# Four of six modulation vectors made by VectorE instead of TensorE in a fused transformer block

## Chip, cores and metric

One core of a Trainium2 chip (trn2). The metric is the device time of one execution in microseconds (us). PE is TensorE, DVE is VectorE, ACT is ScalarE, POOL is GpSimd and SP is SyncE, which here only issues DMAs.

## What is computed

A block of 2048 tokens of width 512: attention over a sliding window of 256 keys with 32 heads of 16, then a gated feed-forward layer of width 1792. Both halves are steered by six vectors of 512 numbers that are made from one condition `c`.

```
mod = (_silu(c) @ w_mod).reshape(1, 6, 1, -1)      # c: 1 x 512, w_mod: 512 x 3072
sa, ca, ga, sb, cb, gb = mod[:, 0], ..., mod[:, 5]
h = _layernorm(x) * (1 + ca) + sa
x = x + ga * attention(h, wqkv, wo)
h = _layernorm(x) * (1 + cb) + sb
x = x + gb * swiglu(h, w1, w3, w2)
```

In the kernel the six vectors are numbered j = 0 to 5 in this order. Vectors 0 and 1 are needed at once, since the first LayerNorm feeds all that follows. Vectors 3 and 4 are needed in the second half of the run, and the gates 2 and 5 when `wo` and `w2` are multiplied by them (the first of these some 130 us into the run).

## The kernel before

The features lie on the 128 partitions in KC = 4 chunks (k = 0 to 3), the tokens in NB = 4 blocks of 512 (b = 0 to 3). All matrix products are made from float32 parts in three passes (`hT` and the weights have a high and a low part each).

The run has an opening of about 57 us, then a long attention phase, then the feed-forward phase. Only the opening is touched by the change. In it the kernel loads x, makes the LayerNorm of each block of tokens (`ln1`, line 632), turns the normed tokens to features on partitions (PE, line 649), applies scale and shift and splits into two parts (`mod_split`, lines 362 to 368: ACT makes `h`, DVE makes both parts of `hT`), makes the values (`values`, line 663, PE products at line 671) and the first queries and keys (`unit_a`, line 442, PE products at line 451), and sends the rows of queries and keys by DMA into the tile `ring` (line 474), in three row groups r = 0, 1, 2 of two DMAs each. Group 0 is cut from the product by ACT (line 460), groups 1 and 2 are finished by two subtractions on POOL (line 469). The scores of a unit (line 504, on PE) read all three groups from `ring`; DVE takes the largest of each row (line 511).

The order is written out by hand. Each step is handed to `at(t, fn)` with a time in an arbitrary unit, the list is sorted, and the functions are called in that order (lines 725 to 727). So each engine has one fixed sequence of instructions, and it waits in place for whatever the next one needs. The dictionary `W` on line 44 holds the times: `mr` and `mm` for the modulation, `ml` for its loads. Each DMA queue is one such sequence too: a DMA whose data is not ready holds back every DMA that SP has behind it.

A modulation vector is made in four steps by `modulation(j, s, t0, at)` (line 578). `row` (line 586): four products of the condition (32 equal columns, `sc32`) with the four chunks of the weight, each on its own 32 rows of the result, 8 matmul instructions since each float32 product runs as two. `out`: ACT copies the 128 x 512 result to SBUF in two pieces (line 596). `turn`: PE sums the four row groups and brings the result to where it is needed. For vectors 0, 1, 3 and 4 that is four products with one column each, result on the partitions (line 604, 8 matmul instructions). For the gates 2 and 5 it is one product of 512 columns, result a row (line 601, 2 matmul instructions). `end`: for 0, 1, 3 and 4 DVE writes `modc` (line 613); for 2 and 5 ACT copies the row (line 610), and SP writes it to DRAM as one row of `g_dr` (line 611), from which it is read back later, spread over the partitions (line 875).

The weights of the modulation go through `stage`, three places of 4 x 128 x 512 that lie inside the still unused part of `vS` (lines 559 to 564). Place 0 holds `wv` (line 625), place 2 vector 0 and place 1 vector 1; then 3 goes to place 2, 4 to place 1, 2 to place 2 and 5 to place 1 (line 717).

Vectors 0 and 1 are made before anything else. The four others are made between the products of `values` and `unit_a`.

Of the kernel before, what the change touches and what calls it, by code (L numbers as in the profile page):

```python
# [16 lines left out]
S, D, F = 2048, 512, 1792  # L17
H, DH = 32, 16
P = 128
KC = D // P  # L20
# [23 lines left out]
W = dict(m=0.15, s=0.1, a=0.29, t=0.541, p=0.377, vs=1.762, vo=0.422, wq=(-1.8, 1.47, 1.5), wv0=-1.811, wvh=(-0.7, -0.65, -0.6, -0.55), wvl=(-0.5, -0.31, -0.3, -0.25), wp=1, A0=2.1, h0=0.539, h=6, hb=6.874, ls=3.287, la=1.146, rf=(1.55, 1.56, 8.4), v=2, vt=1.75, mr=(-1.85, 1.55), mm=(2.6, 4.625, 5.85, 9.2), ml=(-1.79, 1.25, 2.0, 4.9), A=1.268, At=7.876, B=10.4)  # L44
MXB = 3
STB = 3
MODL = 'CECECECE'
# [226 lines left out]
def us(t):  # L274
# [28 lines left out]
def block_kernel(ctx: ExitStack, tc: tile.TileContext, x, wqk, wv, wo, w13, w2, c, wmod, out):  # L303
    nc = tc.nc

    cst = ctx.enter_context(tc.tile_pool(name="cst", bufs=1))
# [6 lines left out]
    o32 = cst.tile([P, P], F32, name="o32")  # L313
# [234 lines left out]
    p0 = pre.enter_context(tc.tile_pool(name="p0", bufs=1, reuse_waits="tile"))  # L548
# [29 lines left out]
    def modulation(j, s, t0, at):  # L578

        v = {}  # L580

        def bank(n):
            v[n] = psA.tile([P, BT], F32, name="mx", bufs=MXB)
            return v[n]

        def row():

            ps = bank(0)
            for k in range(KC):
                nc.tensor.matmul(ps[32 * k:32 * k + 32, :], sc32[:, k], stage[:, s, k], start=True,  # L590
                                 stop=True)

        def out():
            v["e"] = p0.tile([P, D], F32, name="h32", bufs=3)
            for n in range(2):
                nc.scalar.activation(v["e"][:, n * 256:n * 256 + 256], v[0][:, n * 256:n * 256 + 256], AF.Copy)

        def turn():
            ps = bank(1)
            if j in (2, 5):  # L600
                nc.tensor.matmul(ps[:32], o32[:, :32], v["e"], start=True, stop=True)
                return
            for n in range(KC):
                nc.tensor.matmul(ps[:, n:n + 1], v["e"][:, n * P:(n + 1) * P], o32[:, 0:1],
                                 start=True, stop=True)

        def end():
            if j in (2, 5):
                r = p0.tile([P, D], F32, name="h32", bufs=3)
                nc.scalar.activation(r[:1], v[1][:1], AF.Copy)  # L610
                nc.sync.dma_start(g_dr[j // 5:j // 5 + 1, :], r[:1, :])
            else:
                nc.vector.tensor_scalar_add(modc[:, (0, 1, 0, 2, 3)[j]], v[1][:, :KC],
                                            float(j in (1, 4)))

        for n, fn in enumerate((row, out, turn, end)):
            at(h0 + W["mr"][j // 3] if n == 0 and j in (0, 3) else t0 + W["m"] * n, fn)

    wvh = p0.tile([P, KC, D], F32R, name="wvh")
    wvl = p0.tile([P, KC, D], F32R, name="wvl")  # L620

    def load_wv(k, n):
# [5 lines left out]
        else:  # L628
            eng = nc.gpsimd if k < W["wp"] else nc.vector
            eng.tensor_tensor(out=wvl[:, k], in0=raw, in1=wvh.bitcast(F32)[:, k], op=ALU.subtract)  # L630
# [56 lines left out]
    def at(t, fn, kind=None):  # L687
        ops.append((t, len(ops), fn, kind))

    h0 = -40.0  # L690
# [16 lines left out]
    t0 = h0 + 1  # L707
    for b in range(1, NB):
        h = h0 + W["h"] + W["hb"] * (b - 1)
# [820 lines left out]
    n = 0  # L1530
    for half in range(2):
        for p in range(NP):
            k = tf + fl * n
# [80 lines left out]
```

## Time and profile before

| | us |
|---|---|
| median of 3 runs | 972.15 |
| the three runs | 971.44, 972.15, 975.17 |
| span of the profiled execution, first to last instruction | 971.3 |
| PE busy in that span | 942.4 |
| DVE busy | 734.9 |
| ACT busy | 557.1 |
| POOL busy | 538.2 |

The page gives no time of its own for the profiled execution beside its span of 971.3 us; the lowest of the three runs lies 0.1 us above that span, the median 0.85 us. Times inside the run are counted from the start of the span. In the timeline a row gives start, duration, engine, line, operation, operands, how many instructions were merged, and in brackets how long the engine had been idle and what ended that. Durations of PE overlap, since matmuls are pipelined.

### The profile page before, as it was taken

How to read it: one execution, taken by the hardware profiler on the slowest of the kernel's cores; microseconds unless marked ns; L12 is line 12 of the kernel's file. 1: busy time of each engine (PE TensorE's matmuls, PEld its weight loads, DVE VectorE, ACT ScalarE, POOL GpSimd, SP SyncE). 2: the span in 40 equal slices, each digit the busy share in tenths (PEclk: the TensorE clock that was granted, in tenths of full speed). 3: DMA queues.
4: the chain of work that ended last, by engine and by line, in shares of the span. 5: the costliest groups of instructions: out<-in, count | busy, mean ns of one | idle time of the engine just before them, and what ended most of it. 6: DMA issues, size and time to landing. Idle time of an engine off the chain costs nothing.

```text
span 971.3 us, 17150 instructions
## 1 busy us (share of the span) xinstructions
PE 942.4 (97%) x5316; PEld 717.5 (74%) x5316; DVE 734.9 (76%) x2034; ACT 557.1 (57%) x1258; POOL 538.2 (55%) x740
## 2 busy tenths in 40 slices
PE   6999999999999999998998999999999999999998
PEld 3678777777767776775577888888887888888886
DVE  7575889998989998999278686666679766677545
ACT  3333878787878787876578843433456343433330
POOL 8321777787868786865546765337759332222320
PEclk9999999999999999999898999999999999999999
DMA  9521354444544444435795564467654433222102
GB/s 317 170 77 36 134 182 143 144 143 144 176 143 143 144 144 143 133 128 174 211 243 139 194 217 151 142 206 249 194 195 165 141 119 94 63 65 72 44 23 87
DMA packets 80672, 141.65 MB, mean 146 GB/s; under 512 B 9538, under 2 KB 22338, under 8 KB 80580
## 3 DMA queue, kind: packets, MB, share of 16 engines
q1 hardware_dynamic: 79860, 139.50, 44.6%
q10 hardware_dynamic: 720, 1.05, 0.3%
q8 instruction: 42, 0.69, 0.3%
q14 instruction: 50, 0.41, 0.1%
HBM read 85.72 MB, written 34.61 MB: 124 GB/s over the span
## 4 chain that ended last, share of the span: by engine, by line
PE 83%; POOL 5%; DVE 4%; DMA 3%; issue 2%; ACT 2%; SPq 1%; POOLq 0%; DVEq 0%; ACTq 0%
PE st L1384 13%; PE mx L1384 11%; PE pj L451 7%; PE mx L504 7%; PE mx L1478 7%; PE st L763 7%; PE st L1478 7%; PE po L739 6%; PE pj L1384 5%; PE st L671 3%; PE pj L1478 2%; PE mx L1120 2%; POOL pt L791 2%; PE st L1120 2%; POOL qk L469 2%
## 5 line engine op out<-in xcount | busy, mean ns | idle before, releaser
L511 DVE CUSTOM_DVE_ANT_0 junk<-mx,mskq 128x384 bf16<-128x384 f32 (+2 forms) x512 | 256.3, 527 | 28.8 <-PE mx L504 27.2
L504 PE MATMUL mx<-ring 96*128 96x384 f32 (+2 forms) x512 | 154.9, 340 | 6.0 <-DMA ring<-qk 2.4
L763 PE MATMUL st<-ring 100*128 100x384 f32 (+2 forms) x512 | 155.3, 345 | 2.2 <-ACT pt L784 1.2
L791 POOL TENSOR_SCALAR_AFFINE_SELECT pt<-pt 128x256 f32<-128x256 f32 x268 | 109.3, 411 | 63.1 <-ACT pt L784 52.5
L451 PE MATMUL pj<-hT,wq 128*128 128x512 f32 x384 | 136.2, 404 | 1.2 <-DVE wq L440 0.8
L504 PEld LDWEIGHTS mx<-ring 96*128 96x128 f32 x512 | 93.5, 189 | 39.7 <-DVE mt L511 25.8
L784 ACT ACTIVATE pt<-st 128x256 f32<-128x256 f32 x268 | 96.1, 386 | 41.8 <-DVE st L781 33.8
L763 PEld LDWEIGHTS st<-ring 100*128 100x128 f32 x512 | 95.5, 190 | 23.7 <-issue 8.4
L739 PE MATMUL po<-pt,vS 128*17 128x384 f32 (+2 forms) x1408 | 98.6, 398 | 1.7 <-POOL pt L791 1.0
L469 POOL TENSOR_TENSOR qk<-qkr,qk 128x512 fp32r<-128x512 f32 x64 | 83.3, 1302 | 27.6 <-ACT qkr L457 27.4
L976 POOL TENSOR_TENSOR w<-w,w 128x512 fp32r<-128x512 f32 (+2 forms) x36 | 59.8, 1679 | 62.0 <-ACT w L975 44.6
L1428 POOL TENSOR_TENSOR t<-t,t 128x512 f32<-128x512 f32 x28 | 39.7, 1418 | 93.5 <-DVE t L1416 91.7
L781 DVE COPY_PREDICATED st<-later,st 128x128 f32<-128x128 uint8 x268 | 72.2, 291 | 17.4 <-PE st L763 14.5
L451 PEld LDWEIGHTS pj<-hT,wq 128*128 128x128 f32 x384 | 71.4, 190 | 10.2 <-issue 1.7
L739 PEld LDWEIGHTS po<-pt,vS 128*17 128x17 f32 x1408 | 33.5, 98 | 48.4 <-issue 22.4
L1384 PE MATMUL st<-b,w 128*128 128x512 f32 x258 | 64.1, 390 | 0.0
L775 ACT ACTIVATE pt<-st 128x384 f32<-128x384 f32 (+2 forms) x128 | 52.7, 434 | 18.8 <-DVE st L771 12.4
L1416 DVE TENSOR_TENSOR t<-st,t 128x512 f32<-128x512 f32 x52 | 35.7, 686 | 36.4 <-PE st L1384 31.2
L808 POOL TENSOR_SCALAR_AFFINE_SELECT sm<-sm 128x256 f32<-128x256 f32 x109 | 42.1, 409 | 27.9 <-ACT sm L798 25.2
L1456 ACT ACTIVATE wq<-g 128x512 fp32r<-128x512 f32 x28 | 17.8, 634 | 67.5 <-PE st L1478 40.7
L1384 PE MATMUL mx<-b,w 128*128 128x512 f32 x222 | 56.0, 390 | 0.0
L1384 PEld LDWEIGHTS st<-b,w 128*128 128x128 f32 x258 | 48.4, 188 | 10.2
(270 smaller groups left out, 2083.1 us busy)
## 6 DMA issues: line engine op xcount, KB each, us to landing
ring<-qk SPq DMA_DIRECT2D x192, 128.0 KB
o_dr<-os SPq DMA_DIRECT2D x32, 256.0 KB
w<-wsum SPq DMA_DIRECT2D x14, 512.0 KB
w<-w2g SPq DMA_DIRECT2D x14, 512.0 KB
jb<-in_w SPq DMA_DIRECT2D x24, 256.0 KB
wraw<-in_w SPq DMA_DIRECT2D x7, 768.0 KB
w<-wraw SPq DMA_DIRECT2D x14, 384.0 KB
vS<-in_wmod SPq DMA_DIRECT2D x20, 256.0 KB
```

The lines of the kernel that those rows point to most:

```text
L451: nc.tensor.matmul(v["ps"], WQ[g][w][:, n // 3], hTp(i, n // 3, b * BT, BT), start=(n == 0), stop=(n == 3 * KC - 1))
L469: nc.gpsimd.tensor_tensor(out=v[n], in0=v["raw"], in1=v[1].bitcast(F32), op=ALU.subtract)
L504: nc.tensor.matmul(v[i][:, :n], queries(NS, a, gq, 1), keys(NS, hh, a, k0, gq + 1 - k0), start=True, stop=True)
L511: nc.vector.tensor_tensor_reduce(out=junk[:, :n], in0=v[i][:, :n], in1=mskq[:, 3 * P - n:], scale=1.0, scalar=-3e38, op0=ALU.add, op1=ALU. ...
L739: nc.tensor.matmul(po[32 * i:32 * i + DH + 1, qb * P:(qb + nq) * P], vS[:, kb, 4 * g + i], pts[i // 2][:, i % 2, c0:c0 + nq], start=first, ...
L763: nc.tensor.matmul(ps[:, :nq], keys(NM, hh, a, kb, 1), queries(NM, a, kb, nq), start=True, stop=not plus)
L781: nc.vector.copy_predicated(ps[:, 0], later, ps[:, 2])
L784: nc.scalar.activation(held[u, j, a][:, hh, :2], v[j, a, hh][:, :2], AF.Exp, scale=SCALE)
L791: nc.gpsimd.affine_select(out=pt[:, :, 2 * m], in_=pt[:, :, 0], **w)
L976: sch.op(eng, lambda: on_eng(eng).tensor_tensor(out=lo(), in0=src(), in1=hi().bitcast(F32), op=ALU.subtract), tt(eng, n), key, kl + kh, kl ...
L1384: nc.tensor.matmul(ps(bk), WT[s, n][w][:, col], BB[t, k][r], start=start and c == 0, stop=stop and c == 5, skip_group_check=True)
L1478: nc.tensor.matmul(ps(bk), tiles[hk + (h,)][:, i * P:(i + 1) * P], w2_of(last, y, f), start=(m == 0), stop=(m == 5))
```

## The change

Vectors 0 and 1 are made as before. For vectors 3, 4, 2 and 5 the weight is stored transposed in DRAM (`wmodt`): an output on each partition, the 512 inputs along the row. The condition is loaded a second time, spread over all 128 partitions (`load_c`, 128 x 512), into the chunk of `stage` that held the last piece of `wv`, and ACT applies Silu to it in place (`silu_c`). Each chunk of each vector is then one DVE instruction (`cols`): multiply the 128 x 512 weight by the condition and sum along the row, which leaves the result on the partitions. An accumulator read follows it as an instruction of its own. That makes 16 sums in place of four times `row`, `out`, `turn` and `end`. The gates now lie on the partitions (`gatec`, 128 x 4) and go to `g_dr` by a DMA that writes 512 single numbers. The loads of the weights move as well: those of vectors 2 and 5 now stand behind two loads of x and wait for the sums of vectors 3 and 4, whose places they take.

```diff
...
+         hb=6.874, ls=3.287, la=1.146, rf=(1.55, 1.56, 8.4), v=2, vt=1.75, mr=(-1.85,), mm=(3.2, 3.21, 5.73,
+         5.74, 5.75, 5.76, 5.77, 5.78, 8.1, 8.11, 8.12, 8.13, 10.0, 10.01, 10.8, 10.81), ml=(-1.79, 1.25, 6.0,
+         6.4), cr=(-0.2, 1.3), A=1.268, At=7.876, B=10.4)
...
+    gatec = cst.tile([P, 2, KC], F32, name="gatec")
...
         def turn():
             ps = bank(1)
-            if j in (2, 5):
-                nc.tensor.matmul(ps[:32], o32[:, :32], v["e"], start=True, stop=True)
-                return
             for n in range(KC):
...
         def end():
-            if j in (2, 5):
-                r = p0.tile([P, D], F32, name="h32", bufs=3)
-                nc.scalar.activation(r[:1], v[1][:1], AF.Copy)
-                nc.sync.dma_start(g_dr[j // 5:j // 5 + 1, :], r[:1, :])
-            else:
-                nc.vector.tensor_scalar_add(modc[:, (0, 1, 0, 2, 3)[j]], v[1][:, :KC],
-                                            float(j in (1, 4)))
+            nc.vector.tensor_scalar_add(modc[:, j], v[1][:, :KC], float(j))
...
+    crep = stage[:, 0, KC - 1]
+
+    def load_c():
+        nc.sync.dma_start(crep, crow.to_broadcast([P, D]))
+
+    def silu_c():
+        nc.scalar.activation(crep, crep, AF.Silu)
+
+    def home(j, k):
+        return stage[:, 2 if j in (2, 3) else 1, k]
+
+    def load_cols(j):
+        for k in range(KC):
+            nc.sync.dma_start(home(j, k), wmodt[j - 2, :, k])
+
+    def cols(j, k):
+
+        to = modc[:, j - 1, k:k + 1] if j in (3, 4) else gatec[:, j // 5, k:k + 1]
+        nc.vector.tensor_tensor_reduce(out=home(j, k), in0=home(j, k), in1=crep, scale=1.0, scalar=0.0,
+                                       op0=ALU.mult, op1=ALU.add, accum_out=to)
+
+    def cols_end(j):
+        if j == 4:
+            nc.vector.tensor_scalar_add(modc[:, 3], modc[:, 3], 1.0)
+        elif j != 3:
+            nc.sync.dma_start(g_dr[j // 5].rearrange("(k p) -> p k", p=P), gatec[:, j // 5])
...
-    for n, (j, s) in enumerate(((3, 2), (4, 1), (2, 2), (5, 1))):
-        at(h0 + W["ml"][n], lambda j=j, s=s: load_mod(j, s, nc.sync))
-        modulation(j, s, h0 + W["mm"][n], at)
-    at(h0 + W["mm"][3] + 3.1 * W["m"], ones)
+    at(h0 + W["cr"][0], load_c)
+    at(h0 + W["cr"][1], silu_c)
+    for n, j in enumerate((3, 4, 2, 5)):
+        at(h0 + W["ml"][n], lambda j=j: load_cols(j))
+        for k in range(KC):
+            at(h0 + W["mm"][KC * n + k], lambda j=j, k=k: cols(j, k))
+        at(h0 + W["mm"][KC * n + KC - 1] + 0.01, lambda j=j: cols_end(j))
+    at(h0 + W["mm"][-1] + 0.1, ones)
```

Below, rows of the program's order give the line, the operation and its operands, and in brackets the semaphores that the instruction waits for. The rows of the kernel before have its line numbers, those of the changed kernel have its own.

The first place is on ACT, where the first block of tokens is given its scale and shift (`h<-st,modc`, one row for each of the four chunks) and the first weight of the queries is copied (`wq`). The changed kernel has:

```order
L370 ACTIVATE h_242<-st,modc 128x512 [waits DVE_49,PE_49]
L370 ACTIVATE h_251<-st,modc 128x512 [waits PE_49,Activation_49]
L370 ACTIVATE h_260<-st,modc 128x512 [waits PE_49,Activation_49]
L621 ACTIVATE vS<-vS 128x512 [waits DMAHW0_49]
L370 ACTIVATE h_278<-st,modc 128x512 [waits DVE_49,PE_49,Activation_49]
L441 ACTIVATE wq_282<-wqr 128x512 [waits DMAHW1_49]
```

The fourth row, `silu_c`, is new. It stands between the third and the fourth chunk and waits for the DMA that spreads the condition; before, the fourth chunk followed the third directly.

The second place is on SP, where the three row groups of unit 0 are sent to `ring`. Before (`h_414` is the row of gate 2, `h_519` that of gate 5):

```order
L611 DMA g_dr<-h_414 1x512 [waits DMAHW0_49,Activation_49]
L474 DMA ring<-qk_430 16x4x512 [waits DMAHW1_49,Activation_49,Pool_49]
L474 DMA ring<-qk_430 16x4x512 [waits DMAHW2_49,Pool_49]
L474 DMA ring<-qk_433 16x4x512 [waits DMAHW3_49,Pool_49]
L474 DMA ring<-qk_433 16x4x512 [waits DMAHW4_49]
L556 DMA xt<-in_x 128x512 [waits DMAHW5_49,DVE_49,PE_49]
L556 DMA xt<-in_x 128x512 [waits DMAHW6_49,DVE_49,PE_49]
L474 DMA ring<-qk_459 16x4x512 [waits DMAHW7_49,Pool_49]
L474 DMA ring<-qk_459 16x4x512 [waits DMAHW0_49]
L432 DMA wqr<-in_wqk 128x512 [waits DMAHW1_49]
L611 DMA g_dr<-h_519 1x512 [waits DMAHW2_49,Activation_49]
```

And in the changed kernel, from the second row group on:

```order
L479 DMA ring<-qk_404 16x4x512 [waits DMAHW3_49,Pool_49]
L479 DMA ring<-qk_404 16x4x512 [waits DMAHW4_49]
L561 DMA xt<-in_x 128x512 [waits DMAHW5_49,PE_49]
L561 DMA xt<-in_x 128x512 [waits DMAHW6_49,PE_49]
L640 DMA g_dr<-gatec 128x4x1 [waits DMAHW7_49,DVE_49]
L479 DMA ring<-qk_430 16x4x512 [waits DMAHW0_49,Pool_49]
L479 DMA ring<-qk_430 16x4x512 [waits DMAHW1_49]
L437 DMA wqr<-in_wqk 128x512 [waits DMAHW2_49]
L640 DMA g_dr<-gatec 128x4x1 [waits DMAHW3_49,DVE_49]
```

The write of gate 2 has moved from ahead of the first row group to just ahead of the third, and it now waits for DVE.

The third place is on DVE, where the second block of tokens is split (`hT`, here its last two chunks) and the statistics of the third block follow (`BN_STATS`). The changed kernel has:

```order
L372 CAST hT<-h_447 128x512 [waits Activation_49]
L373 TENSOR_TENSOR hT<-h_447,hT 128x512 [waits DVE_49]
L633 ISA vS,gatec<-vS 128x512 [waits DMAHW1_49]
L633 ISA gatec 128x1
L633 ISA vS,gatec<-vS 128x512 [waits DMAHW2_49]
L633 ISA gatec 128x1
L633 ISA vS,gatec<-vS 128x512 [waits DMAHW3_49]
L633 ISA gatec 128x1
L633 ISA vS,gatec<-vS 128x512 [waits DMAHW4_49]
L633 ISA gatec 128x1
L358 BN_STATS bst<-xt 128x6 [waits DMAHW7_49]
```

The four sums of gate 2 (each with its accumulator read) stand behind the last chunk of the split and ahead of the statistics; before, nothing stood between these. Of the other sums, two stand ahead of the scaling of the second block's tokens (line 358 before), six behind it, three behind the statistics of the third block, and the last between the first two row maxima.

More of the change, by code (lines that the diff above doesn't have):

```diff
@@ L43 @@
 MODE = 'CDCPCCCP'
-W = dict(m=0.15, s=0.1, a=0.29, t=0.541, p=0.377, vs=1.762, vo=0.422, wq=(-1.8, 1.47, 1.5), wv0=-1.811, wvh=(-0.7, -0.65, -0.6, -0.55), wvl=(-0.5, -0.31, -0.3, -0.25), wp=1, A0=2.1, h0=0.539, h=6, hb=6.874, ls=3.287, la=1.146, rf=(1.55, 1.56, 8.4), v=2, vt=1.75, mr=(-1.85, 1.55), mm=(2.6, 4.625, 5.85, 9.2), ml=(-1.79, 1.25, 2.0, 4.9), A=1.268, At=7.876, B=10.4)
+W = dict(m=0.15, s=0.1, a=0.29, t=0.541, p=0.377, vs=1.762, vo=0.422, wq=(-1.8, 1.47, 1.5), wv0=-1.811,
+         wvh=(-0.7, -0.65, -0.6, -0.55), wvl=(-0.5, -0.31, -0.3, -0.25), wp=1, A0=2.1, h0=0.539, h=6,
+         hb=6.874, ls=3.287, la=1.146, rf=(1.55, 1.56, 8.4), v=2, vt=1.75, mr=(-1.85,), mm=(3.2, 3.21, 5.73,
+         5.74, 5.75, 5.76, 5.77, 5.78, 8.1, 8.11, 8.12, 8.13, 10.0, 10.01, 10.8, 10.81), ml=(-1.79, 1.25, 6.0,
+         6.4), cr=(-0.2, 1.3), A=1.268, At=7.876, B=10.4)
 MXB = 3
@@ L302, in block_kernel @@
 @with_exitstack
-def block_kernel(ctx: ExitStack, tc: tile.TileContext, x, wqk, wv, wo, w13, w2, c, wmod, out):
+def block_kernel(ctx: ExitStack, tc: tile.TileContext, x, wqk, wv, wo, w13, w2, c, crow, wmod, wmodt, out):
     nc = tc.nc
@@ L607, in end @@
         def end():
-            if j in (2, 5):
-                r = p0.tile([P, D], F32, name="h32", bufs=3)
-                nc.scalar.activation(r[:1], v[1][:1], AF.Copy)
-                nc.sync.dma_start(g_dr[j // 5:j // 5 + 1, :], r[:1, :])
-            else:
-                nc.vector.tensor_scalar_add(modc[:, (0, 1, 0, 2, 3)[j]], v[1][:, :KC],
-                                            float(j in (1, 4)))
-        for n, fn in enumerate((row, out, turn, end)):
-            at(h0 + W["mr"][j // 3] if n == 0 and j in (0, 3) else t0 + W["m"] * n, fn)
+            nc.vector.tensor_scalar_add(modc[:, j], v[1][:, :KC], float(j))
+        for n, fn in enumerate((row, out, turn, end)):
+            at(h0 + W["mr"][0] if n == 0 and j == 0 else t0 + W["m"] * n, fn)
+    crep = stage[:, 0, KC - 1]
[17 more added lines that the diff above has]
+            nc.sync.dma_start(g_dr[j // 5].rearrange("(k p) -> p k", p=P), gatec[:, j // 5])
     wvh = p0.tile([P, KC, D], F32R, name="wvh")
@@ L1603 @@
         "c": con(np.asarray(c).reshape(KC, P).T),
-        "wmod": con(np.asarray(w_mod).reshape(KC, P, 6, D).transpose(2, 1, 0, 3)),
+        "crow": con(np.asarray(c).reshape(1, D)),
+        "wmod": con(np.asarray(w_mod)[:, :2 * D].reshape(KC, P, 2, D).transpose(2, 1, 0, 3)),
+        "wmodt": con(np.asarray(w_mod)[:, 2 * D:].reshape(D, 4, KC, P).transpose(1, 3, 2, 0)),
     }
```

## The prediction

> **What bounds the kernel now.** I read the page first: engine totals, then the chain of work that ended last.
>
> ```profile
> span 971.3 us, 17150 instructions
> PE 942.4 (97%) x5316; PEld 717.5 (74%) x5316; DVE 734.9 (76%) x2034; ACT 557.1 (57%) x1258; POOL 538.2 (55%) x740
> PE 83%; POOL 5%; DVE 4%; DMA 3%; issue 2%; ACT 2%; SPq 1%; POOLq 0%; DVEq 0%; ACTq 0%
> ```
>
> PE holds 83% of the chain, so work taken from PE shortens the run if PE does not then wait. The change lies in the opening, so the next view is the windows of 20 us there (length; then busy time of PE, PEld, DVE, ACT, POOL; clock; DMA).
>
> ```profile
> 20.00:40.00 20.00, 18.73 (x96) 12.48 (x96) 10.01 (x25) 7.00 (x16) 5.50 (x7) 1.00 0.58 194
> 40.00:60.00 20.00, 19.57 (x96) 13.95 (x94) 15.10 (x37) 8.80 (x16) 11.30 (x11) 1.00 0.34 111
> ```
>
> PE is full and DVE has 15 us free in these 40, so moving the sums to DVE can pay. Third, the chain in order of time tells which of the removed products lie on it.
>
> ```profile
> 22.30 0.70 DVE wq L440
> 23.04 0.50 PE pj L451
> 23.77 0.79 PE mx L604 x8
> 28.15 0.99 PE mx L590 x8
> 30.27 0.79 PE mx L604 x8
> 33.02 1.00 PE mx L590 x8
> 35.34 0.99 PE mx L601 x2
> 43.97 1.12 PE mx L590 x8
> ```
>
> Up to 23.0 us the chain ran on DVE. From there it is PE nearly throughout, and all removed products but the first row of vector 3 are in it. Last, I read the timeline of each engine around the new waits.
>
> **What is removed.** PE's timeline:
>
> ```profile
> 17.46 2.03 PE L590 MATMUL mx<-vS,sc 128*32 128x512 f32 x8
> 20.33 0.50 PE L451 MATMUL pj<-hT,wq 128*128 128x512 f32 x1 [0.41 <-ACT wq L436]
> 23.04 0.50 PE L451 MATMUL pj<-hT,wq 128*128 128x512 f32 x1 [0.81 <-DVE wq L440]
> 34.51 0.60 PE L649 MATMUL st<-ident,xt 128*128 128x128 f32 x4
> 45.87 1.04 PE L601 MATMUL mx<-h,o 128*32 128x512 f32 x2 [0.26 <-ACT h L596]
> 49.04 0.22 PE L504 MATMUL mx<-ring 96*128 96x128 f32 x1
> ```
>
> The row of vector 3 at 17.46 is hidden: PE waits for ACT and DVE until 23.04 anyway. The others on the chain are 0.79 + 0.99 + 0.79 + 1.00 + 0.99 + 1.12 + 1.04 = 6.72, with the wait of 0.26 about 7.0 us, all ahead of the first score at 49.04. ACT loses eight short copies and two rows, off the path but for one named below. If nothing else moved, the span would be 964.3.
>
> **First new wait: the spread condition.** Its DMA overwrites the last chunk of wv, so it goes out when DVE has made the third piece of `wvl`. ACT's fourth chunk `h` stands behind `silu_c`.
>
> ```profile
> 15.38 2.32 DVE L630 TENSOR_TENSOR wvl<-vS,wvh 128x512 fp32r<-128x512 f32 x3
> 18.98 0.78 ACT L365 ACTIVATE h<-st,modc 128x512 f32<-128x512 f32 x1 [0.82 <-DVE hT L368]
> 130.00 0.57 SPq L875 DMA_DIRECT2D wqr<-g_dr  x1
> 133.72 1.32 POOL L880 TENSOR_TENSOR jb<-jb,wqr 128x512 f32<-128x512 f32 x1 [0.28 <-DMA wqr<-g_dr]
> ```
>
> The DMA goes out at 15.38 + 2.32 = 17.7. The nearest row for its landing is the other DMA that spreads a row of 512 over the partitions: issued at 130.00, waited for until 133.72, so 3.7 us. No other load of the opening can bound it below; at best it lands when the fourth chunk wants ACT anyway (18.98 less one Silu, no loss), at worst at 21.4. I take 21.2, near the row. A 128x512 step of ACT follows (0.55 from start to start), so `h` starts at 21.8 and not at 18.98, the first weight at 22.5, its product at 23.1 and not at 20.33. Between that product and the one at 23.04 PE had 2.71 - 0.81 = 1.9 us of work, so the latter now starts at 25.0: **+2.0**. DVE is late by 1.5 (its last split from 21.12 to 22.6).
>
> **The clock.** PE now stands almost still from about 19.2 to 23.1. What a pause does to the clock is shown later in the run (window, length, PE busy, granted clock, DMA):
>
> ```profile
> 66.72:70.13 3.41, 2.87 (x14) 1.00 0.00 0
> 452.42:455.84 3.42, 2.43 (x14) 1.00 0.69 221
> 455.84:459.25 3.41, 3.41 (x26) 0.50 0.88 238
> 517.28:520.69 3.41, 1.42 (x12) 1.00 1.06 264
> 520.69:524.10 3.41, 2.64 (x6) 0.50 0.48 177
> 524.10:527.52 3.42, 3.42 (x11) 0.50 0.00 0
> ```
>
> The clock is granted in stretches of 3.41 us. After one with PE busy for 2.43 or 1.42 the next ran at half, after one with 2.87 it did not; a half-speed stretch with only 2.64 was followed by another. A pause of 3.9 us leaves some stretch under 2.43, so a half-speed one follows, which loses up to 1.7; I take **+1.4** (0 to 3.1).
>
> The Trainium skill, in "TensorE: Matmul & The Clock Gate", Part 1, says that the clock falls to half after at least one idle window of about 3.4 us and comes back after one busy window. No stretch quoted here is idle, and two of them were followed by half speed, so the trace is the stricter; by the page a pause of 3.9 us need not hold a whole idle window, and this term and the later one like it could be 0.
>
> **The sums on DVE.** The nearest instruction is the same operation at the same width (by form):
>
> ```profile
> L991 DVE CUSTOM_DVE_ANT_0 x1b<-mx,x1b 128x512 f32<-128x512 f32 x5 | 3.4, 682 | 0.2 <-PE mx L1120 0.2
> 37.64 0.43 DVE L367 CAST hT<-h 128x512 fp32r<-128x512 f32 x1 [5.02 <-ACT h L365]
> 36.35 0.59 ACT L610 ACTIVATE h<-mx 1x512 f32<-1x512 f32 x1 [1.49 <-PE mx L601]
> 36.85 0.76 ACT L365 ACTIVATE h<-st,modc 128x512 f32<-128x512 f32 x1
> 39.87 3.20 POOL L469 TENSOR_TENSOR qk<-qkr,qk 128x512 fp32r<-128x512 f32 x2 [12.30 <-ACT qkr L457]
> 41.96 1.66 DVE L368 TENSOR_TENSOR hT<-h,hT 128x512 fp32r<-128x512 f32 x1
> 44.29 0.69 DVE L368 TENSOR_TENSOR hT<-h,hT 128x512 fp32r<-128x512 f32 x1
> ```
>
> 0.68 each, 0.61 from start to start with the accumulator read inside, so 16 are 9.8 us. Beside POOL's L469 a two-operand step of DVE took 1.66 and not 0.69; I take 0.61, since POOL is past L469 when the sums that matter run (bounds 0.61 and 1.66). The first eight fall into DVE's idle 5.02 us. They would end near 34.7. PE's transposes of block 1 move from 34.51 by +2.0 + 1.4 - 3.6 (four removed pieces) = -0.2 to 34.3, and ACT's chunk follows 0.6 later without line 610, which held it before; DVE gets it at 35.7, so these eight cost nothing, with 1.0 to spare. The split of block 1 ended at 44.9 (44.29 + 0.69, less an overlap of 0.1); now it ends at 44.9 - 0.2 - 1.7 = 43.0 (1.7 is ACT's row of line 610 and the product of line 601, which stood between these transposes).
>
> **Second new wait: gate 2 ahead of the third row group.** Now DVE makes the four sums of gate 2: 43.0 + 2.45 = 45.4. SP waits for them to write `g_dr`, and the third row group is queued behind that.
>
> ```profile
> 44.08 1.20 SPq L474 DMA_DIRECT2D ring<-qk  x2
> L535 SPq DMA_DIRECT2D ring<-mT x64: 659/684/755, 73.2 to 462.3; - x64
> 0.79 0.41 ACTq L550 DMA_DIRECT2D c_sb<-in_c  x1
> 4.11 1.28 ACT L573 ACT_TABLE_LOAD   x1 [4.11 <-DMA c_sb<-in_c]
> ```
>
> The issue of a write of this many dimensions takes about 0.7 (L535), so the two DMAs of the row group go out from 46.2 to 47.4, where they went from 44.08 to 45.28. The landing: under 49.04 - 45.28 = 3.8 after the issue, since the score did not wait; c's small load landed within 4.11 - 1.20 = 2.9. I take 2.5, so 49.9. Ahead of them in the queue are 512 pieces of 4 bytes. c's load is 128 pieces; of its 2.9 the pieces are an unknown part, so four times as many add anything from 0 to 8.7, and the likely part is small, since most of such a time is there for any DMA. I take 0.3, so the first score at 50.2 and not 49.04: **+1.2**. PE would be there at 49.04 + 3.4 - 7.0 = 45.4. It waits 4.8 us: all seven microseconds are given back here. And a pause of 4.8 us means another half-speed stretch, **+1.4** to 1.7.
>
> **The rest.** The sums of gate 5 (2.4 us of DVE) stand among the statistics and first row maxima. DVE is through with three of them at 43.0 + 2.45 + 3.4 + 0.1 + 1.8 = 50.8, about when the first maximum can start (50.4); it holds nothing by more than 0.4, inside the wait above. Two loads of x go behind the second write, 15 us before they are read. After 49 us PE and DVE take turns on the chain without slack, so what is lost stays lost.
>
> Sum: +1.2 + 1.4 and 0.2 for the maxima = +2.8 us. On the span 971.3 that is 974.1; the median lies 0.85 above the span, so **975.0 us**, slower by 0.3%.
>
> **Rivals.** A measurement of this kernel can tell about 0.5% (4.9 us) from no change, so the borders are 967.3 and 977.0.
>
> (a) *The scatter holds the queue.* If the 512 pieces take 4 us more than I allow, the third row group lands at 54.2, the pause is 9 us, the half-speed stretch follows: +1.2 + 4 + 1.7 = +6.9, 979 us. It decides from 2 us on. For it: no row here shows 4-byte writes to DRAM, and c's 128 pieces already cost up to 2.9. Against: that figure holds the fixed part. The same price comes if the sums run at 1.66 beside POOL: 4 x 1.05 = 4.2. In the Trainium skill, "DMA: Bandwidth & Descriptors", Specifications, transfers under 512 bytes are done as read-modify-write; no run here shows one, and no time follows from it.
>
> (b) *The clock does not fall.* Then block 1's transposes come 1.4 earlier, DVE's eight sums become the limit (34.7), the row group goes out 1.0 earlier, and the second half-speed stretch is gone: 1.2 - 1.0 + 0.2 = +0.4, 972.6. Against it stand the windows above. The page's rule on an idle window would give this.
>
> (c) *The third row group is not held,* because DVE is done before POOL has the group. Then PE keeps 7.0 less the first wait of 2.0: -5.0, 967.1, and with an earlier landing of the condition up to -7, 965. Against it: the order has the four sums and the write ahead of the group, and POOL was done in time for 44.08 before. It needs the split of block 1 to end 3 us earlier than I find.
>
> **How the numbers follow.** My forecast 0.44, (b) 0.18, (a) 0.27, (c) 0.11. Forecast and (b) lie within 0.5%: 0.62; slower 0.27; faster 0.11. The range from 968 to 980 leaves out most of (c) and the far end of the scatter, under 2 in 10 together.
>
> **What would show it.** Right: ACT idle before `silu_c` until 21 us, a row of 0.50 in the granted clock near 23 and near 50, the write of `g_dr` issued after 45 us on SP and directly behind it the row group, and the first score with 4 to 5 us of PE idle in front of it, ended by the DMA of `ring`. Wrong: that score at 43 to 46 us with no wait (c), the score after 53 us or sums of over 1 us each (a), or a clock of 1.00 throughout (b). I would also be wrong if PE's later stretches held slack, so that a late first score were caught up by 100 us.

## The result and the profile after

The changed kernel takes 979.34 us (median of six runs, 977.42 to 980.00) against 971.80 for the kernel before (six runs beside it, 970.16 to 975.17). The ratio is 1.0078, with a 95% interval of 1.0062 to 1.0094: slower by 0.8%. The profiled execution took 980.0 us, with a span of 978.3.

The page first: span, engine totals, and the shares of the chain that ended last.

```profile
span 978.3 us, 17059 instructions
PE 930.3 (95%) x5264; PEld 717.3 (73%) x5264; DVE 744.8 (76%) x2065; ACT 552.6 (56%) x1249; POOL 539.4 (55%) x740
PE 78%; DMA 7%; DVE 6%; POOL 5%; issue 2%; ACT 2%; SPq 1%; POOLq 0%; DVEq 0%; ACTq 0%
```

PE has 12.1 us less to do (942.4 before), yet the span grew by 7.0, and the DMAs' share of the chain went from 3% to 7%. The timeline of PE shows where it stood still.

```profile
24.04 0.80 PE L456 MATMUL pj<-hT,wq 128*128 128x512 f32 x1 [5.16 <-ACT wq L441]
35.39 0.60 PE L672 MATMUL st<-ident,xt 128*128 128x128 f32 x4
45.39 0.40 PE L694 MATMUL st<-wvh,hT 128*128 128x512 f32 x1
57.12 0.45 PE L509 MATMUL mx<-ring 96*128 96x128 f32 x1 [11.34 <-DMA ring<-qk]
```

The first product with `wq` comes at 24.04 (20.33 before), the last product ahead of the first score ends at 45.8, and the score itself waits 11.3 us for rows of `ring` and starts at 57.12 (49.04 before). ACT and SP (for SP: the issue of its DMAs) name the two waits.

```profile
22.17 0.63 ACT L621 ACTIVATE vS<-vS 128x512 f32<-128x512 f32 x1 [3.88 <-DMA vS<-in_crow]
```

```profile
17.88 0.33 SPq L618 DMA_DIRECT2D vS<-in_crow  x1
...
46.76 0.39 SPq L640 DMA_DIRECT2D g_dr<-gatec  x1
47.24 1.21 SPq L479 DMA_DIRECT2D ring<-qk  x2
48.50 0.58 SPq L437 DMA_DIRECT2D wqr<-in_wqk  x1
```

Silu of the spread condition starts 4.3 us after its load went out. Gate 2's 512 numbers go out at 46.76 and the third row group right behind, until 48.45; the score that needs it starts 8.7 us after that. The trace's records of the DMAs show what went on in between. The 512 packets of 4 bytes start between 47.7 and 48.0 and take 7 to 9 ns each, and the row group's packets of 2 KB follow until 50.0. Then the DMA engines move nothing for 2.4 us (windows of the whole core; the last two columns are the DMA share and GB/s):

```profile
48.40:50.00 1.60, 0.00 (x0) 0.00 (x0) 1.50 (x5) 0.00 (x0) 0.00 (x0) 0.97 0.54 174
50.00:52.40 2.40, 0.00 (x0) 0.00 (x0) 1.97 (x7) 0.00 (x0) 1.32 (x1) 0.50 0.00 0
```

Each DMA here reports 16 completions, and it has landed when the last is in. Those of the write come between 53.83 and 56.67, so it lands 9.9 us after its issue; the two DMAs of the row group land just behind it, at 56.85 and 57.03. In the kernel before, the row group had landed at 47.77, 3.1 us after the issue of its second DMA.

DVE made the numbers like this:

```profile
35.92 0.69 DVE L633 CUSTOM_DVE_ANT_0 vS<-vS 128x512 f32<-128x512 f32 x1
...
43.59 0.69 DVE L373 TENSOR_TENSOR hT<-h,hT 128x512 fp32r<-128x512 f32 x1
44.20 0.69 DVE L633 CUSTOM_DVE_ANT_0 vS<-vS 128x512 f32<-128x512 f32 x1
```

A sum takes 0.61 from start to start; the eighth ends at 36.6, gate 2's four run from 44.20 to 46.7. Last, the windows around PE's two pauses (length; busy time and instructions of PE; granted clock; DMA):

```profile
19.00:22.40 3.40, 0.00 (x0) 1.00 0.68 230
22.00:25.40 3.40, 1.36 (x3) 0.59 1.03 386
25.40:28.80 3.40, 3.40 (x9) 0.50 0.33 127
49.90:53.30 3.40, 0.00 (x0) 0.50 0.14 23
60.10:63.50 3.40, 3.40 (x10) 0.50 0.31 32
```

Half speed held from 22.6 to 29.4, and again from 49.9 to 63.5, of which PE worked through the last 6.4 us.

**How the lead of PE developed.** PE runs the same instructions in the same order in both kernels, but for the removed ones. So each matmul can be found in both traces, and the difference of its start says how far one kernel is behind the other at that point. Against the kernel before, in us, at the matmul which starts there at the time given:

| | 20.3 | 36.3 | 48.6 | 55.1 | 100 | 200 | 260 | 540 | 967 |
|---|---|---|---|---|---|---|---|---|---|
| changed kernel | +3.7 | -0.2 | -3.4 | +11.1 | +11.0 | +15.4 | +17.0 | +13.0 | +7.1 |

Two things stand in this row. The opening costs 11 us, not 3. And from 540 us to the end the changed kernel gains 5.9 us, in a part of the run that the change does not touch. (It gains 4.0 between 260 and 540 us too; but three kernels tried below, which are the kernel before with one more write, gain 1.8 to 2.9 there against the same trace, so much of that lies in this one execution of the kernel before.) The second part had to be understood before the end times could say anything of the first.

### The profile page after: what moved, and what is told of

It reads as the page before. It is cut to its first block, busy times and chain, and to the rows that moved or that the text cites. A ratio compares the mean times of both kernels' runs of the same rounds, so it can differ in the third digit from the quotient of the medians.

```text
span 978.3 us, 17059 instructions
## 1 busy us (share of the span) xinstructions
PE 930.3 (95%) x5264; PEld 717.3 (73%) x5264; DVE 744.8 (76%) x2065; ACT 552.6 (56%) x1249; POOL 539.4 (55%) x740
## 4 chain that ended last, share of the span: by engine, by line
PE 78%; DMA 7%; DVE 6%; POOL 5%; issue 2%; ACT 2%; SPq 1%; POOLq 0%; DVEq 0%; ACTq 0%
PE st L1411 12%; PE mx L1411 10%; PE pj L456 8%; PE mx L509 7%; PE st L790 7%; PE mx L1505 6%; PE po L766 6%; PE st L1505 6%; PE pj L1411 5%; PE st L694 4%; DMA ring<-qk 2%; PE pj L1505 2%; POOL qk L474 2%; POOL pt L818 2%; PE mx L1147 1%
## 5 line engine op out<-in xcount | busy, mean ns | idle before, releaser
L766 PE MATMUL po<-pt,vS 128*17 128x384 f32 (+2 forms) x1408 | 96.5, 390 | 3.1 <-POOL pt L818 2.8
```

Of the source, the lines that this page charges most:

```text
L766: nc.tensor.matmul(po[32 * i:32 * i + DH + 1, qb * P:(qb + nq) * P], vS[:, kb, 4 * g + i], pts[i // 2][:, i % 2, c0:c0 + nq], start=first, ...
```

## The experiments

Each kernel was timed beside runs of the kernel before on the same chip; ratios are against those (medians 970.38 to 971.04).

### Silu of the condition later

```diff
-         6.4), cr=(-0.2, 1.3), A=1.268, At=7.876, B=10.4)
+         6.4), cr=(-0.2, 1.52), A=1.268, At=7.876, B=10.4)
```

> Silu of the condition is put one place later on ScalarE, behind the copy of wq, and nothing else moves. Theory (the 512 four-byte pieces of gate 2's write hold the third row group of the ring; the condition's wait is the smaller loss): the first product is back near 20.3 us instead of 24.04, the half-speed stretches at 22.6 to 29.4 go, PE is done with block 1 some 4 to 5 us earlier, but the row group lands some 9.5 us behind its issue all the same. The sums on VectorE (start 29.4 in the changed kernel) move with PE, so gate 2's write goes out some 4 us earlier and the first score with it: about 53 us in place of 57.1, and the time 974 to 976. Rival (the whole loss is the condition's wait and its clock): 970 to 972, first score at or below 50.

Measured: 978.4 us, ratio 1.0076 (1.0062 to 1.0091). PE's timeline:

```profile
20.26 0.51 PE L456 MATMUL pj<-hT,wq 128*128 128x512 f32 x1 [1.57 <-ACT wq L441]
35.21 0.66 PE L672 MATMUL st<-ident,xt 128*128 128x128 f32 x4 [0.18 <-ACT h L370]
52.85 0.45 PE L509 MATMUL mx<-ring 96*128 96x128 f32 x1 [11.67 <-DMA ring<-qk]
```

The first wait is gone (20.26; one of its two half-speed stretches stayed), the score comes at 52.85 as the theory said, and its own wait is as long as in the changed kernel, 11.67. But the time did not follow: 4 us won at the score were worth 1 us at the end. The expectation of 974 to 976 missed for that reason.

### Gate writes later

```diff
-        at(h0 + W["mm"][KC * n + KC - 1] + 0.01, lambda j=j: cols_end(j))
+        at(h0 + (W["mm"][KC * n + KC - 1] + 0.01 if n < 2 else (8.9, 15.95)[n - 2]), lambda j=j: cols_end(j))
```

> The writes of gates 2 and 5 are put just behind the third row group's and behind the next unit's rows in SyncE's queue; the condition's wait stays. Theory: the third row group lands 2.5 to 3.5 us behind its issue instead of 9.7, the first score starts at 48 to 50 us and not at 57.1, and the time is 970 to 973, against 979.3 for the changed kernel. If the pieces hold whatever is behind them, the loads behind gate 2's write land late as well, which may cost up to 3 us of that. Rival (the score is late because PE and VectorE are late, not because of the write): the score stays at 55 or more and the time at 977 to 980.

Measured: 974.13 us, ratio 1.0034 (1.0016 to 1.0051). First PE, then ACT:

```profile
46.46 0.33 PE L509 MATMUL mx<-ring 96*128 96x128 f32 x1 [1.46 <-DMA ring<-qk]
...
60.38 0.66 PE L672 MATMUL st<-ident,xt 128*128 128x128 f32 x4 [2.21 <-ACT h L370]
```

```profile
59.03 0.63 ACT L441 ACTIVATE wq<-wqr 128x512 fp32r<-128x512 f32 x1 [5.43 <-DMA wqr<-in_wqk]
```

With the write behind it, the row group is in time: the score starts at 46.46 with a wait of 1.5. Now the next load behind the write is late, `wqr` (issued at 46.40, right after the write at 45.95), and ACT waits 5.4 us for it. The write holds whatever stands behind it. The score came earlier than the expected 48 to 50 us; the time missed the expected 970 to 973, by less than the 3 us that late loads were said to cost.

### Both edits

```diff
-         6.4), cr=(-0.2, 1.3), A=1.268, At=7.876, B=10.4)
+         6.4), cr=(-0.2, 1.52), A=1.268, At=7.876, B=10.4)
...
-        at(h0 + W["mm"][KC * n + KC - 1] + 0.01, lambda j=j: cols_end(j))
+        at(h0 + (W["mm"][KC * n + KC - 1] + 0.01 if n < 2 else (8.9, 15.95)[n - 2]), lambda j=j: cols_end(j))
```

> Both edits: Silu of the condition behind the copy of wq, and the two gate writes behind the row groups. Theory: both losses of the changed kernel go and the removed 6.7 us of TensorE show: first score at 43 to 46 us (before: 49.04), time 965 to 968, below the kernel before at 971.8. Rival (what was removed from TensorE lay beside a limit further on, the loads of the ring or VectorE, so that it buys nothing): first score not below 48, time 970 to 973.

Measured: 969.15 us, ratio 0.9979 (0.9964 to 0.9993), between the two expectations. The score starts at 43.77, within the theory's range, but PE then waits elsewhere:

```profile
43.77 0.33 PE L509 MATMUL mx<-ring 96*128 96x128 f32 x1 [0.94 <-DMA ring<-qk]
...
57.92 0.66 PE L672 MATMUL st<-ident,xt 128*128 128x128 f32 x4 [1.93 <-ACT h L370]
```

### Rows of 512 bytes at the same place

TensorE turns the columns, ScalarE copies them, and SP writes four rows; gate 2's write keeps its place in the queue.

```diff
+    def gate_turn(j):
+        gt[j] = psA.tile([P, BT], F32, name="mx", bufs=MXB)
+        nc.tensor.transpose(gt[j][:KC, :P], gatec[:, j // 5], ident)
...
+        nc.sync.dma_start(g_dr[j // 5].rearrange("(k p) -> k p", p=P), gt[j][:KC, :P])
```

> As the changed kernel, with gate 2's write at the same place in SyncE's queue, but TensorE first turns the gate's 128x4 columns to 4x128 and ScalarE copies them, so that the write has 4 rows of 512 bytes and not 512 pieces of 4. Gate 5 is turned and written at a later free place, and the condition's wait stays. Theory (the number of pieces is the price): the third row group lands 2.5 to 3.5 us behind its issue, first score 50 to 51.5, time 972 to 974.5. Rival (the price is the place in the queue, with the wait for VectorE's sums): score at 55 or more, time 978 to 981.

Measured: 969.49 us, ratio 0.9991 (0.9979 to 1.0004). SP and PE:

```profile
47.44 0.33 SPq L652 DMA_DIRECT2D g_dr<-h  x1
47.86 1.21 SPq L479 DMA_DIRECT2D ring<-qk  x2
```

```profile
46.68 0.37 PE L644 MATMUL mx<-ident,gatec 128*4 128x128 f32 x1 [5.34 <-DVE gatec L633]
```

The row group goes out 0.6 later than in the changed kernel and nothing waits for it: its second DMA lands at 51.04, 2.6 us after its issue, and the score shows no wait. (The score comes at 52.5, later than the expected 50 to 51.5, since PE itself waited 5.3 us for DVE's sums before the turn.) So the place in the queue, with its wait for DVE, is not what cost 8 us. The time came out below the theory, for the reason that the next experiment shows.

### The kernel before, with 32 bytes more

```diff
     modc = cst.tile([P, 4, KC], F32, name="modc")
+    cst.tile([P, 8], F32, name="pad")
```

> The kernel before with one unused tile of 32 bytes a partition among its constants, where the changed kernel has its gate columns. Every instruction and its order stay; all tiles on the left of the local memory lie 32 bytes further up. Theory (from 540 us on all five changed kernels run the same TensorE instructions some 6 us faster than the kernel before; the matmuls that pair a left and a right tile take 0.389 there and 0.395 to 0.396 before, and the new tile of 32 bytes is what shifted them): 965 to 967.5, no gain before 540 us. Rival (the drift comes from something else that the change does, or differs from run to run): 970 to 972.

Measured: 965.33 us, ratio 0.9933 (0.9911 to 0.9956). No instruction differs from the kernel before; the tile is never used. Three groups of matmuls by line and form, between 560 and 900 us, in the kernel before, and then in this one (busy time in us, mean ns of one):

```profile
L1384 PE MATMUL st<-b,w 128*128 128x512 f32 x192 | 47.5, 389 | 0.0
L1384 PE MATMUL st<-b,wo 128*128 128x512 f32 x162 | 41.2, 395 | 0.0
...
L1384 PE MATMUL mx<-b,o 128*128 128x512 f32 x138 | 34.1, 396 | 0.0
```

```profile
L1385 PE MATMUL st<-b,w 128*128 128x512 f32 x203 | 50.3, 389 | 0.0
L1385 PE MATMUL st<-b,wo 128*128 128x512 f32 x156 | 38.6, 389 | 0.0
L1385 PE MATMUL mx<-b,o 128*128 128x512 f32 x138 | 33.2, 390 | 0.2 <-DVE x1a L1484 0.2
```

The matmuls that read `b` with `wo` or `o` went from 395 and 396 ns to 389 and 390; those that read `b` with `w` stayed at 389. In the program's addresses `b` and `w` lie on the left side of the local memory and move with the new tile, from multiples of 64 bytes to 32 bytes past them; `wo` and `o` lie on the right, do not move, and stand 32 bytes past such a multiple. So do `qk`, `qkr` and `wq`, which are read with `w`. These behave in two ways (again the kernel before, then this one):

```profile
L1478 PE MATMUL mx<-w,wq 128*128 128x512 f32 x96 | 24.8, 395 | 0.0
L1478 PE MATMUL mx<-w,qk 128*128 128x512 f32 x90 | 24.7, 396 | 0.0
```

```profile
L1479 PE MATMUL mx<-w,wq 128*128 128x512 f32 x96 | 24.7, 394 | 0.0
L1479 PE MATMUL mx<-w,qk 128*128 128x512 f32 x92 | 24.6, 390 | 0.0
```

With `qk` the mean fell by 6 ns too, with `wq` only by 1. So the place of the tiles matters, but not every matmul becomes fast when its two places agree. By the offset of PE this kernel gains 6.0 us from 540 us to the end. There are 588 matmuls of `b` with `wo` or `o` in that part and 312 of `w` with `qk` or `qkr`; from start to start they gain 5.3 of these 6.0 us.

### The changed kernel, with 32 bytes more

```diff
     gatec = cst.tile([P, 2, KC], F32, name="gatec")
+    cst.tile([P, 8], F32, name="pad")
```

> The changed kernel with another unused tile of 32 bytes, so that the left tiles stand 64 bytes further up than before. Theory of the placement: the matmuls of the second half are back at 0.395, and the run loses the gain: 983.5 to 986. Rival (placement means nothing): 978 to 980.

Measured: 985.47 us, ratio 1.0141 (1.0115 to 1.0166).

```profile
L1412 PE MATMUL st<-b,wo 128*128 128x512 f32 x162 | 41.2, 395 | 0.0
L1412 PE MATMUL mx<-b,o 128*128 128x512 f32 x138 | 34.1, 396 | 0.0
```

The left tiles are back at multiples of 64 bytes, and the matmuls back at 395. So placement is shown, in both directions, and the change is 14 us slower at equal placement: 1.0141 - 1 = 1.4% with the old one, 1.0078 - 0.9933 = 1.45% with the new one.

### The pieces alone, in the kernel before

```diff
+    at(h0 + W["rf"][2] - 0.01, lambda: nc.sync.dma_start(spare[0].rearrange("(k p) -> p k", p=P), ident[:, :KC]))
```

> The kernel before with one more DMA: four columns of a constant are written as 512 pieces of four bytes to a spare tensor in device memory, on SyncE directly ahead of the third row group of the ring. Nothing waits for it and it waits for nothing. Theory (the pieces hold the DMAs behind them for some 9 us): the third row group lands at 53.5 to 55 instead of 47.8, the first score starts at 54 to 55 with 5 us of idle TensorE ahead, a half-speed stretch may follow, and the time is 976 to 979. Rival (the pieces are cheap by themselves and the hold comes from writing what VectorE has just made): first score at 49 to 50, 971 to 972.5.

Measured: 979.85 us, ratio 1.0079 (1.0053 to 1.0105). SP and PE:

```profile
43.83 0.42 SPq L722 DMA_DIRECT2D spare<-ident  x1
44.34 1.19 SPq L475 DMA_DIRECT2D ring<-qk  x2
```

```profile
56.94 0.45 PE L505 MATMUL mx<-ring 96*128 96x128 f32 x1 [7.94 <-DMA ring<-qk]
```

One unneeded DMA of 2 KB, which waits for nothing, puts the score at 56.94. This DMA lands 12.5 us after its issue, at 56.29, and the row group behind it at 56.84. The theory is shown: the pieces alone cost 8.8 us (971.04 to 979.85). That this is also the changed kernel's time is chance, since that kernel has the late condition as well and gains some 6 us by its placement. The score came some 2 us later than the expected 54 to 55. The expected time of 976 to 979 was a little low, also because half speed held until 62.1 us (granted clock 0.50 from 51.9 on), and PE fell back by a further 2.4 behind the score.

### 128 pieces of 16 bytes

```diff
-    at(h0 + W["rf"][2] - 0.01, lambda: nc.sync.dma_start(spare[0].rearrange("(k p) -> p k", p=P), ident[:, :KC]))
+    at(h0 + W["rf"][2] - 0.01, lambda: nc.sync.dma_start(spare[0].rearrange("(p k) -> p k", p=P), ident[:, :KC]))
```

> As the kernel before with the extra write of 2 KB ahead of the third row group, but the spare tensor is laid out so that each partition's four numbers lie together: 128 pieces of 16 bytes in place of 512 of 4. In the run with 512 pieces the first score came at 56.94 against 49.04. Theory (the price goes by the number of pieces, some 18 ns each): a quarter of the hold of 7 to 9 us, so the first score at 50 to 51.5 and 971.5 to 974. Rival (any write of pieces that small pays one price for the whole DMA): first score at 55 or more and 977 or more.

Measured: 970.74 us, ratio 1.0001 (0.9986 to 1.0015).

```profile
49.36 0.22 PE L505 MATMUL mx<-ring 96*128 96x128 f32 x1
```

No wait at all; both expectations missed, the theory by 1 us and the rival by 6. This write lands 4.0 us after its issue, against 12.5 with 512 pieces. A quarter of the pieces costs far less than a quarter. The run changes their number and their size together, and also whose numbers lie side by side in device memory, so which of these matters stays open.

### The pieces on another queue

```diff
-    at(h0 + W["rf"][2] - 0.01, lambda: nc.sync.dma_start(spare[0].rearrange("(k p) -> p k", p=P), ident[:, :KC]))
+    at(h0 + W["rf"][2] - 0.01, lambda: nc.scalar.dma_start(spare[0].rearrange("(k p) -> p k", p=P), ident[:, :KC]))
```

> The same extra write of 512 pieces of 4 bytes in the kernel before, but issued by ScalarE, on its queue, some 3 us ahead of the third row group. Theory A (the hold is the order within SyncE's queue): the row group lands as before, first score at 49 to 49.5, 970 to 972.5. Theory B (the 16 DMA engines themselves are held, whichever queue the pieces come from): first score at 52 to 55, 974 to 978.

Measured: 981.28 us, ratio 1.0111 (1.0088 to 1.0133). ACT's queue, then PE:

```profile
42.68 0.39 ACTq L722 DMA_DIRECT2D spare<-ident  x1
```

```profile
57.25 0.45 PE L505 MATMUL mx<-ring 96*128 96x128 f32 x1 [6.64 <-DMA ring<-qk]
```

The score comes at 57.25: worse than theory B's 52 to 55, and far from A. SP's DMAs are held by pieces that stand in another queue: the seven that SP issues from 43.09 to 46.74 take 11.0 to 11.7 us to land, where the kernel before shows 2.2 to 3.3.

### The pieces into local memory

```diff
     modc = cst.tile([P, 4, KC], F32, name="modc")
+    pad = cst.tile([P, 8], F32, name="pad")
...
+    at(h0 + W["rf"][2] - 0.01, lambda: nc.sync.dma_start(pad[:, 0:8:2], ident[:, :KC]))
```

> The kernel before with the 32-byte tile (965.3 by itself), and a DMA of 512 pieces of 4 bytes at the same place of SyncE's queue, but into that tile, every other column of it, and so into local memory and not device memory. Theory A (stores of 4 bytes to device memory are what is slow): first score within 1.5 us of 49.3, 965 to 967.5. Theory B (the number of pieces is slow wherever they go): first score at 55 to 57.5, 971.5 to 975.

Measured: 963.39 us, ratio 0.9935 (0.9913 to 0.9956), the ratio of the kernel with the unused tile.

```profile
49.05 0.22 PE L505 MATMUL mx<-ring 96*128 96x128 f32 x1
```

512 pieces of 4 bytes at the same place of the same queue cost nothing when they go to local memory; this DMA lands 3.7 us after its issue. It is their storing in device memory that is slow.

### Rows of 512 bytes, late, and Silu late

The edits of the first and the fourth experiment together, with both gates turned, copied and written some 5 us after DVE has them:

```diff
-        tq = h0 + (W["mm"][KC * n + KC - 1] + 0.01 if n < 3 else 12.0)
+        tq = h0 + (W["mm"][KC * n + KC - 1] + 0.01 if n < 2 else 12.0 + 0.1 * n)
```

> The changed kernel with Silu of the condition behind the copy of wq, and both gates turned on TensorE, copied by ScalarE and written as four rows of 512 bytes, behind the third row group and some 5 us later than VectorE makes them, so that neither TensorE nor the queue waits. Theory (opening and placement add up): first score near 43.5, no later hold, TensorE 5 to 6 us ahead of the kernel before at 100 us, and with the gain of the second half 960 to 963. Rival (something between 50 and 65 us, as the statistics of the next block, sets the pace there whatever comes first): at 100 us level with the kernel before, 965 to 968.

Measured: 966.07 us, ratio 0.9948 (0.9924 to 0.9973): the rival's range.

```profile
44.59 0.33 PE L509 MATMUL mx<-ring 96*128 96x128 f32 x1 [3.46 <-DMA ring<-qk]
48.81 0.33 PE L509 MATMUL mx<-ring 96*128 96x128 f32 x1 [0.37 <-DVE mt L516]
50.76 0.27 PE L644 MATMUL mx<-ident,gatec 128*4 128x128 f32 x1 [0.39 <-DVE mt L516]
```

PE is early and waits: 3.5 us for the row group and then, by turns, for the row maxima. At equal placement it stands even with the kernel before (966.07 against 965.33 with the unused tile, intervals overlapping). The profiled execution took 962.91, 3 us less than the median, so its row in the table below is better than the median would be.

### Five more DMAs

```diff
+    for n in range(5):
+        at(h0 + 9.5, lambda n=n: nc.sync.dma_start(spare[n:n + 1], ident[:1, :]))
```

> The kernel with late rows of 512 bytes for both gates and Silu behind the copy of wq, plus five writes of 512 bytes each to a spare tensor at a time when SyncE's queue is idle. The changed kernel has 458 DMAs on SyncE against 455 before, and all kernels with its opening wait for ring rows near 180 to 196 us (1.7 to 1.8 us) and near 230 to 246, which those with the opening of before don't. Theory (each DMA takes the next of eight completion counters, and the shift by three makes other DMAs wait on each other; five more make it a shift by eight): the wait near 181 us goes and the time is 962 to 965. Rival (it has another cause): the wait of 1.7 stays, and 965 to 967.

Measured: 964.96 us, ratio 0.9941 (0.9920 to 0.9963).

```profile
180.76 0.43 PE L510 MATMUL mx<-ring 96*128 96x384 f32 x1 [1.89 <-DMA ring<-qk]
```

The wait near 181 us stayed (1.7 without the five DMAs, 1.9 with them). The time lies on the border of the two expected ranges and does not separate them, but the wait does: the theory of the counters falls. The cause of these waits stays open.

**The offsets at equal placement.** Against the kernel before with the unused tile, in us, at the matmul that starts there at the time given (apart from the line numbers, all six differ from it by the changed opening alone):

| | 20.7 | 36.1 | 48.7 | 55.2 | 100 | 200 | 260 | 540 | 959 |
|---|---|---|---|---|---|---|---|---|---|
| changed kernel | +3.4 | -0.5 | -3.7 | +10.9 | +10.9 | +15.1 | +16.5 | +14.9 | +15.0 |
| Silu late | -0.4 | -5.1 | -8.3 | +6.1 | +6.1 | +10.2 | +13.3 | +13.8 | +13.8 |
| writes late | +3.2 | -1.3 | -4.5 | -1.4 | +3.8 | +7.6 | +8.2 | +7.4 | +7.4 |
| both | +0.1 | -3.5 | -6.7 | -3.6 | +1.0 | +2.8 | +3.7 | +2.5 | +2.6 |
| rows of 512 bytes | +3.6 | -0.6 | +3.1 | +3.3 | +3.3 | +5.4 | +5.6 | +3.1 | +3.1 |
| rows late, Silu late | +0.1 | -5.2 | -8.4 | -2.7 | -2.7 | -1.1 | -0.6 | -2.2 | -2.1 |

From 540 us on each row is constant to 0.1: with the placement equal, nothing in the second half depends on the change.

## Why the prediction was right, and where it was not

The time, 979.3 us, lies inside the range of 968 to 980, but beyond the border of 977.0, and the forecast of 975.0 did not come about. Of the signs that the prediction named, ACT's wait, half speed near 23 and 50 us, and the write behind 45 us are there; but a score after 53 us was its sign for rival (a), and it came at 57.12. At equal placement the time would have been outside the range, 985.5. Step by step:

- **What is removed**, and the lead that it gives. Right. PE was through with its work ahead of the score at 45.8; the prediction had 45.4.
- **The first wait and its clock**, +2.0 and +1.4. The mechanism was right, the size 1 us small: block 1's transposes begin at 35.39, not 34.3. The load of the condition took 4.3 us to Silu, not 3.5, and two half-speed stretches followed, not one. Taking the wait away gives 4.7 us at 55 us (10.85 - 6.13, rounded in the last table), and 1.2 us at the end.
- **The sums on DVE**, 0.61 each and hidden. Right; the eighth ended at 36.6, beside nothing that waited.
- **The second wait: the place in the queue.** Right: the row group went out from 47.24 to 48.45 (forecast 46.2 to 47.4), late by the 1 us of the step above.
- **The second wait: the scatter**, taken as 0.3 within bounds of 0 to 8.7. This step failed. The score came 8.7 us after the row group's last issue, where 2.5 + 0.3 were allowed: the pieces cost 5.9 more than that, 6.2 in all. I reasoned from c's load that most of such a time is there for any DMA; but that load goes into local memory, and 512 pieces into local memory held nothing, as the experiment with them shows, while the same number to device memory took 9.9 to 12.5 us to land. The bound was wide enough, the value chosen near its wrong end. Rival (a) named this mechanism and the point from which it decides, with a size of 4 us; its mechanism is what happened. That its 979 us is also the time measured is an accident, by the last point of this list.
- **The second half-speed stretch**, +1.4. The mechanism was right, the size not: behind the score PE fell back by another 3 us, since the pause was 11 us long and the clock stayed down until 63.5.
- **The maxima and gate 5**, +0.2. The offset does not move between 55 and 100 us. Right.
- **"What is lost stays lost."** Wrong in both directions. Between 100 and 260 us the changed kernel falls back by 5.6 more (last table). PE waits 1.1, 1.8 and 1.9 us for rows of `ring` there, near 139, 196 and 246 us, and the kernel before 0.4; their cause is open. The pieces alone do not bring them: put into the kernel before, they cost 10.4 us at 100 us and 11.0 at 260. And of the 4.7 us that a late Silu saves in the opening, 3.6 are lost again by 540 us.
- **What the prediction did not have at all:** the 32 bytes of `gatec` move the tiles behind it on the left side, and that is worth 5.9 us in the second half. Two errors of opposite sign, some +11 and -6, put the time inside the range.

The Trainium skill, in "DMA: Bandwidth & Descriptors", Specifications, has transfers under 512 bytes done as read-modify-write, and the prediction drew no time from it. The trace agrees only in part: 512 pieces of 4 bytes to device memory held the DMAs for some 8 us, 128 pieces of 16 bytes, also far below 512, for nothing that can be seen. The same page of the Trainium skill, under "Why small descriptors are slow (HBM only)", says that transfers between local memories do not suffer from small descriptors; with that the pieces into local memory agree (score at 49.05, no wait).

On the clock, the pause of the changed kernel held a whole idle window (0.00 us busy from 19.00 to 22.40), and half speed followed at 22.6: there the rule in "TensorE: Matmul & The Clock Gate", Part 1, of the Trainium skill holds as it stands.

Of the expected gain of 7.0 us nothing is left even when both waits are gone. With the rows late and Silu late, PE leads by 8.4 us ahead of the score and by 2.7 right behind it; the lead runs into the row group's own arrival and the row maxima. So most of the removed 7 us lay ahead of another limit.

## What to carry to other kernels

Count the separate runs of bytes that a store to device memory consists of: a column spread over the partitions, written as 4-byte pieces, can cost more than the engine work that it saves, and DMAs of another queue wait for it too. Compare the mean time of unchanged instructions in unchanged parts before judging a change by its end time; a new small tile can move all the tiles behind it. An offset of the same instruction between two traces, followed along the run, separates such effects where the end time adds them up.

## What the runs showed of the hardware

- 512 pieces of 4 bytes stored to device memory hold other DMAs, in the same queue and in another one: the first score, which waits for such rows, came at 56.9 and 57.3 us and not at 49.0. The pieces' own packets all start within 0.4 us, but their DMA lands 9.9 to 12.5 us after its issue, and the row group behind it lands after it. 128 pieces of 16 bytes do not hold them (landed after 4.0), nor do 512 of 4 bytes into local memory (3.7). Whether the number, the size or the arrangement of the pieces decides is open.
- 128x512 matmuls of `b` with `wo` or `o`, and of `w` with `qk` or `qkr`, took 394 to 396 ns in the mean where the places of the two tiles differ by 32 bytes modulo 64, and 389 to 390 where they agree. Those of `w` with `wq` took 393 to 395 either way, so equal places alone do not decide it. Why, and what other shifts do, was not tried.
- Not tried: the changed kernel with its gates written as 16-byte pieces. The fastest kernels were those with the old opening and the unused 32 bytes (965.33, and 963.39 with the harmless extra DMA) and the two with late rows (966.07 and 964.96), which their intervals do not separate.
